# The inverse root of a normalisation on GpSimd by three Newton steps instead of on VectorE, with the sums of squares issued 3 instead of 7 units behind the last products

## The chip, the cores and the metric

The program runs on one core of a Trainium2 chip. A core has a TensorE for matrix products (PE in the profile, its weight loads PEld), VectorE (DVE), ScalarE (ACT), GpSimd (POOL) and SyncE (SP), which here issues every DMA. Each engine works through its own queue in order; an instruction that waits for another engine holds up all that stand behind it on its own. The metric is the device time of one launch in microseconds. Lower is better.

## The reference

Attention by landmarks (Nyström) for 8 batches and 8 heads of 576 tokens with 64 elements, then a normalisation and a gated multi-layer perceptron over the 4608 tokens that come out, all in float32:

```python
def attention(q, k, v):                      # per batch and head
    q_lm, k_lm = means of 18 tokens each     # 32 landmarks
    A, Bm, C = sm(q, k_lm), sm(q_lm, k_lm), sm(q_lm, k)      # softmax, scale 1/8
    Z = Bm.T / (norm_1(Bm) * norm_inf(Bm) + 1e-6)
    for _ in range(6):
        Z = 2 * Z - Z @ Bm @ Z
    return A @ Z @ C @ v

def moe(x, w_gate, w_val, w_out, rms_g):     # x: 4608 x 512, d_ff = 1536
    xn = x / sqrt(mean(x * x, axis=-1) + 1e-6) * rms_g
    g = xn @ w_gate
    return (g * sigmoid(g) * (xn @ w_val)) @ w_out
```

The change is at `1 / sqrt(mean(x * x) + 1e-6)`, one value for each token.

## The kernel before, in words

Each batch `b` (0 to 7, 576 tokens) goes through these stages, written as Python generators that yield between pieces:

- `stage1(b, g)` for the two groups `g` of four heads: VectorE sums landmarks (`lmT`, L342), TensorE makes the scores `sC` and `sA` (a **block** of 32-row matmuls), VectorE takes maxima (L376 to L379) and transposes, ScalarE takes exponentials. Its `back` part makes the rows of A on GpSimd (`tA`, L407 and L414: subtract the maximum, multiply by the inverse sum) and C v on TensorE (`pCV`).
- `newton(b)`: the pseudo-inverse. Six times TensorE multiplies (`pn`) and VectorE updates (`PV`, L498; the last one is `VZ`, L502): a chain that goes to and fro between the two.
- `second(b)`: the attention's output `pO` (the **last products** of the batch), copied by ScalarE to `xr` (L554) and squared (L556). The sums of squares over the 512 channels are matmuls with ones (`pss`, L562), VectorE transposes them (L563), one more matmul adds the four parts (`pms`, L569), and VectorE makes `ms = mean + 1e-6` (L571), a first guess of the inverse root by integer arithmetic (L575, L576), and refines it in **two rounds** of four operations (L578 to L581) on 128 x 18 elements. `Rb` (L583) spreads the root, `Rt` (L585) transposes it, four operations scale `xr` (L587).
- `finish` splits the scaled values into a rounded part `xhi` (ScalarE, L614) and a rest `xlo` (VectorE and GpSimd in turn, L616). A float32 product is made of three fast ones.

The perceptron's first 4 of 12 blocks of 128 hidden channels run while the attention is still going on, in nine **chunks** of 512 tokens (`mlp_chunk`): for each block 12 products `psg` and 12 `psv`, then 48 products `pso` for the output. Chunk `i` needs the split values of batch `i`, and of the batch before for the rest. After the last chunk the other 8 blocks follow in two passes (`Fast`, `unit`), with 7 products in place of 8 for each pair of matrices. Weights are decoded on VectorE and ScalarE from a packed form (L189 to L203).

TensorE's order is the order in which the code issues its matmuls. It is set by `Mixer`, which steps the generators by an estimated clock: each of a chunk's products moves it on by 0.216 units, and a generator that yields `(busy, wait)` goes on when the clock has moved by `busy + wait * slack` (slack 1.8 in the beginning, then 1.3). The constants `OWL0` (batch 0) and `OWL` (the others) are such a wait: between the last products and squares of a batch and its `pss`. On the other engines a scheduler places instructions by its own estimates and by priority. The streams of `second` and `newton` are urgent ones. A chunk is issued only when the batch it needs has been issued in full (`mix.drain`).

Of the kernel before, what the change touches and what calls it, by code (L numbers as in the profile page):

```python
# [13 lines left out]
ALU = mybir.AluOpType  # L14
# [4 lines left out]
P = 128  # L19
# [1 line left out]
NW = 6.0  # L21
NS = 1.0
SLACK0 = 1.8
OWL0 = 7.0
G2 = "newton"
F1 = 1
F2 = 2
# [5 lines left out]
KW2 = 2.5  # L33
OW = 2.0
SQW = 1.5
OWL = 7.0
WW = 2.5
WQ = 0
VM = 0
# [3 lines left out]
RBA = 0  # L43
# [36 lines left out]
def nystrom_moe_kernel(  # L80
# [12 lines left out]
    nc = tc.nc  # L93
# [6 lines left out]
    M = 32  # L100
# [6 lines left out]
    NB = S // M  # L107
# [32 lines left out]
    def mm(*args, **kw):  # L140
        tc.keep_in_program_order(nc.tensor.matmul(*args, **kw))  # L141
# [156 lines left out]
    with tc.tile_pool(name="ap", bufs=1, side="right") as ap, tc.tile_pool(  # L298
# [240 lines left out]
        def second(b):  # L539
            nt = state.pop(b)  # L540
            (Whi, Wlo), ATs = nt["W"], nt["AT"]
            xr = ap.tile([P, NK, S], F32, name="xr", tag="xr", bufs=2)
            sq = ap.tile([P, NK, S], F32, name="sq", tag="sq", bufs=1)
            for g in range(2):
                po = [[pa.tile([P, HS], F32, name="pO", tag="pa") for j in range(2)] for e in range(2)]
                for e in range(2):
                    for n, (w, a) in enumerate(((Whi, 0), (Whi, 1), (Wlo, 0))):
                        for j in range(2):
                            r = slice(j * D, (j + 1) * D)
                            cols = slice(e * HS, (e + 1) * HS)  # L550
                            mm(po[e][j], w[r, g], ATs[g][r, a, cols], start=(n == 0), stop=(n == 2))
                for e in range(2):
                    for j in range(2):
                        nc.scalar.copy(xr[:, 2 * g + j, e * HS : (e + 1) * HS], po[e][j])  # L554
                for kk in (2 * g, 2 * g + 1):
                    nc.scalar.activation(sq[:, kk], xr[:, kk], AF.Square)  # L556
                yield 0.9, ((OWL if b else OWL0) if g == 1 else OW)
            sqT = ap.tile([P, NB, M], F32, name="sqT", tag="sqT", bufs=1)
            for e in range(2):
                pss = pa.tile([P, HS], F32, name="pss", tag="pa")  # L560
                for kk in range(NK):
                    mm(pss[kk * M : (kk + 1) * M, :], ones, sq[:, kk, e * HS : (e + 1) * HS], start=True, stop=True)  # L562
                nc.vector.transpose(  # L563
                    sqT[:, e * (NB // 2) : (e + 1) * (NB // 2), :].rearrange("p n m -> p (n m)"), pss
                )
            yield 1.1, SQW
            part = sqT[:, :, 0]
            pms = pa.tile([P, NB], F32, name="pms", tag="pa")
            mm(pms, sel.rearrange("p g t -> p (g t)"), part, start=True, stop=True)  # L569
            ms = sm.tile([P, NB], F32, name="ms", tag="ms")  # L570
            nc.vector.tensor_scalar(ms, pms, 1.0 / DM, 1e-6, op0=ALU.mult, op1=ALU.add)  # L571
            r1 = sm.tile([P, NB], F32, name="r1", tag="r1")
            r2 = sm.tile([P, NB], F32, name="r2", tag="r2")
            ri = r1.bitcast(I32)
            nc.vector.tensor_single_scalar(ri, ms.bitcast(I32), 1, op=ALU.logical_shift_right)  # L575
            nc.vector.tensor_scalar(ri, ri, -1, 0x5F3759DF, op0=ALU.mult, op1=ALU.add)  # L576
            for c in (1.0, 0.375**2):
                nc.vector.tensor_mul(r2, r1, r1)  # L578
                nc.vector.scalar_tensor_tensor(r2, r2, c, ms, op0=ALU.mult, op1=ALU.mult)
                nc.vector.scalar_tensor_tensor(r2, r2, -10.0 / 3.0, r2, op0=ALU.add, op1=ALU.mult)  # L580
                nc.vector.scalar_tensor_tensor(r1, r2, 5.0, r1, op0=ALU.add, op1=ALU.mult)  # L581
            Rb = ap.tile([P, NB, M], F32, name="Rb", tag="sqT", bufs=1)
            (nc.scalar.mul if RBA else nc.vector.tensor_scalar_mul)(Rb, r1.unsqueeze(2).broadcast_to([P, NB, M]), 0.375**2)  # L583
            Rt = ap.tile([P, S], F32, name="Rt", tag="Rt", bufs=1)
            nc.vector.transpose(Rt, Rb.rearrange("p n m -> p (n m)"))  # L585
            for kk in range(NK):
                last = nc.vector.scalar_tensor_tensor(  # L587
                    xr[:, kk], xr[:, kk], gsb[:, kk : kk + 1], Rt, op0=ALU.mult, op1=ALU.mult
                )
            scaled.append(last.ins)  # L590
            nc.sync.dma_start(x_dram[b], xr)
            xrs[b] = xr
            if HOLD == 2 and b == 0:
                hold.enter_context(tc.issue_after(last.ins))
            finish(b, 0)
            if HOLD == 1 and b == 0:
                hold.enter_context(tc.issue_after(last.ins))
# [4 lines left out]
        def finish(b, which):  # L602
            xr = xrs[b]
            pos = 0
            while pos < S:
                gp = b * S + pos
                i, off = gp // T, gp % T
                n = min(S - pos, T - off)
                if (i > b) != which:
                    pos += n  # L610
                    continue
                xhi, xlo = chunk_tiles(i)
                for kk in range(NK):
                    nc.scalar.copy(xhi[:, kk, off : off + n], xr[:, kk, pos : pos + n])  # L614
                    eng = nc.gpsimd if kk % XLP == XLS else nc.vector
                    eng.tensor_sub(  # L616
                        xlo[:, kk, off : off + n],
                        xr[:, kk, pos : pos + n],
                        xhi[:, kk, off : off + n].bitcast(F32),
                    )  # L620
                pos += n
# [33 lines left out]
        def seconds():  # L655
            for b in range(B):
                while stage["newton"] < b or stage["chunk"] < b - 1:
                    yield -0.3
                yield from second(b)
                stage["second"] = b  # L660
# [393 lines left out]
```

## Time and profile before

| | |
|---|---|
| time, median of 3 runs | 1065.7 us (1065.2 to 1069.69) |
| the profiled execution | 1064.71 us, its span 1062.8 us |
| busy in the span: PE, DVE, ACT, POOL | 993, 743, 487, 90 us |
| granted clock of TensorE, mean | 0.96 |

Times in the profile's views are counted from the start of the span. In the page's strip of 40 slices one slice is 26.6 us and a digit is the busy share in tenths. A row of the timeline gives the start, the time taken, the engine, the source line, the operation, what it writes from what, the shape, and in brackets the idle time of the engine before it with what ended that. Groups give the busy time in total and the mean of one in ns. L141 is the line of the helper that issues every matmul, so that matmuls are told apart by what they write. The last attention batch ends at about 436 us; from there to the end TensorE runs the two passes.

### The profile page before, as it was taken

To read this page: it belongs to the slowest core of one execution; us is meant where nothing else is said; L and a number is where in the kernel's file an instruction comes from. 1 tells how busy PE (TensorE), PEld (TensorE's weight loads), DVE (VectorE), ACT (ScalarE), POOL (GpSimd) and SP (SyncE) were. 2 spreads that over 40 slices of the span, in tenths; PEclk is the share of its full clock that TensorE was granted. 3 is DMA by queue.
4 is the path that set the end of the run, shared out by engine and by line. 5 is a ranking of instruction groups with operands and counts; after the bars stand their busy time and mean duration, and the time that the engine had idled before them with its cause. 6 is when DMAs were issued, how large, how long until landed. Compare 5 with 4: busy or idle time off the path is not lost.

```text
span 1062.8 us, 17582 instructions
## 1 busy us (share of the span) xinstructions
PE 992.8 (93%) x6918; PEld 833.9 (78%) x6918; DVE 743.4 (70%) x1503; ACT 486.7 (46%) x990; POOL 89.5 (8%) x86
## 2 busy tenths in 40 slices
PE   5639689989989999999999999999999999999998
PEld 3326466556767777787989899998999989899997
DVE  7799586797494551988995675747897475675743
ACT  3534556555454543455645352433744334352431
POOL 2243121211020210100000000000000000000000
PEclk7659889999999999999999999999999999999999
DMA  9244343434140211543533505134250432505122
GB/s 335 100 150 136 133 164 105 153 104 163 43 142 11 86 45 40 187 145 119 189 123 135 178 1 179 51 129 155 64 178 21 159 96 83 179 1 178 50 70 80
DMA packets 62946, 123.82 MB, mean 117 GB/s; under 512 B 5520, under 2 KB 27024, under 8 KB 61840
## 3 DMA queue, kind: packets, MB, share of 16 engines
q1 hardware_dynamic: 62864, 122.71, 34.0%
q8 instruction: 54, 0.88, 0.3%
q14 instruction: 28, 0.23, 0.1%
HBM read 84.94 MB, written 37.75 MB: 115 GB/s over the span
## 4 chain that ended last, share of the span: by engine, by line
PE 72%; DVE 15%; DMA 6%; issue 2%; ACT 2%; POOL 2%; SPq 0%; ACTq 0%; POOLq 0%; DVEq 0%
PE pso L141 23%; PE px L141 18%; PE pz L141 9%; PE psg L141 6%; PE psv L141 5%; PE pw L141 5%; DMA qk<-in_q_dram 2%; PE pO L141 2%; DMA srawv<-in_moe_w_val_dram 1%; DVE lmT L342 1%; PE pn L141 1%; DVE xr L587 1%; DVE h L275 1%; PE sC L141 1%; PE pss L141 1%
## 5 line engine op out<-in xcount | busy, mean ns | idle before, releaser
L141 PE MATMUL pso<-whio,h 128*128 128x512 f32 x288 | 96.2, 402 | 5.8 <-DVE h L275 4.7
L141 PE MATMUL pso<-solo,h 128*128 128x512 f32 x432 | 100.4, 390 | 0.0
L829 ACT CAST x<-xf 128x768 fp32r<-128x768 f32 x84 | 68.1, 833 | 69.7 <-DVE xf L847 54.2
L141 PEld LDWEIGHTS pso<-solo,h 128*128 128x128 f32 x432 | 81.0, 188 | 16.3
L141 PE MATMUL pso<-sowhio,h 128*128 128x512 f32 x288 | 90.9, 390 | 0.0
L141 PE MATMUL psg<-xhi,whig 128*128 128x512 f32 x144 | 60.7, 421 | 25.6 <-ACT xhi L614 25.6
L945 DVE TENSOR_TENSOR ob<-ob,pso 128x512 f32<-128x512 f32 x72 | 48.8, 684 | 49.1 <-PE pso L141 48.1
L830 DVE TENSOR_TENSOR x<-xf,x 128x768 fp32r<-128x768 f32 x84 | 79.2, 953 | 5.0 <-ACT x L829 5.0
L877 DVE TENSOR_TENSOR h<-c,h 128x384 fp32r<-128x384 f32 x96 | 53.2, 555 | 37.3 <-ACT h L876 37.2
L898 ACT COPY c<-px 128x384 f32<-128x384 f32 x48 | 23.1, 481 | 108.6 <-PE px L141 108.6
L141 PEld LDWEIGHTS pso<-whio,h 128*128 128x128 f32 x288 | 53.4, 188 | 20.4 <-DVE h L275 6.0
L876 ACT CAST h<-c 128x384 fp32r<-128x384 f32 x96 | 49.4, 515 | 34.5 <-DVE c L887 28.3
L141 PE MATMUL psg<-xlo,whig 128*128 128x512 f32 x144 | 60.6, 421 | 4.7 <-DVE xlo L616 4.0
L141 PEld LDWEIGHTS pso<-sowhio,h 128*128 128x128 f32 x288 | 54.1, 188 | 11.0
L141 PE MATMUL psg<-xhi,wlog 128*128 128x512 f32 x144 | 60.5, 420 | 0.0
L141 PE MATMUL psv<-xhi,wlov 128*128 128x512 f32 x144 | 58.1, 403 | 0.0
L141 PE MATMUL px<-x,swfs0c 128*128 128x384 f32 x288 | 58.0, 335 | 0.0
L141 PE MATMUL psv<-xlo,whiv 128*128 128x512 f32 x144 | 58.0, 403 | 0.0
L141 PE MATMUL px<-x,swfs1c 128*128 128x384 f32 x288 | 57.8, 334 | 0.1
L141 PE MATMUL px<-x,swfs2c 128*128 128x384 f32 x288 | 57.8, 335 | 0.0
L141 PE MATMUL psv<-xhi,whiv 128*128 128x512 f32 x144 | 57.8, 401 | 0.0
L141 PE MATMUL pso<-wloo,h 128*128 128x512 f32 x144 | 57.4, 398 | 0.0
(224 smaller groups left out, 2231.6 us busy)
## 6 DMA issues: line engine op xcount, KB each, us to landing
xd<-xr SPq DMA_DIRECT2D x8, 1152.0 KB, 4.3
pd<-ob SPq DMA_DIRECT2D x36, 256.0 KB, 2.1
xf<-xd SPq DMA_DIRECT2D x8, 1152.0 KB, 7.5
ob<-pd SPq DMA_DIRECT2D x36, 256.0 KB, 3.5
pe<-ob SPq DMA_DIRECT2D x36, 256.0 KB, 2.6
ob<-pe SPq DMA_DIRECT2D x36, 256.0 KB, 2.8
out_dram<-ob SPq DMA_DIRECT2D x36, 256.0 KB, 2.7
vt<-in_v_dram SPq DMA_DIRECT2D x16, 512.0 KB, 4.0
```

The costliest lines, as they stand in the source:

```text
L141: tc.keep_in_program_order(nc.tensor.matmul(*args, **kw))
L275: nc.vector.tensor_sub(h2, s, h1.bitcast(F32))
L342: nc.vector.tensor_reduce(lmT[:, z], qk[z].rearrange("p h (m c) -> p h m c", c=LM), axis=AX.X, op=ALU.add)
L587: last = nc.vector.scalar_tensor_tensor(xr[:, kk], xr[:, kk], gsb[:, kk : kk + 1], Rt, op0=ALU.mult, op1=ALU.mult)
L829: nc.scalar.copy(t[:, 0], src)
L830: nc.vector.tensor_sub(t[:, 1], src, t[:, 0].bitcast(F32))
L876: nc.scalar.copy(hi, s)
L877: nc.vector.tensor_sub(lo, s, hi.bitcast(F32))
L898: nc.scalar.copy(c1, px)
L945: nc.vector.tensor_add(ob, ob, bank.pop(t))
```

## The change

The two rounds on VectorE become three Newton steps on GpSimd, each of four operations, `y = y * (1.5 - 0.5 * ms * y * y)`, twelve in a row where each needs the one before. Rounds of the old kind carried a factor that `Rb` multiplied in; the new ones don't, so `Rb` is a plain copy. `OWL0` and `OWL` go from 7 to 3.

```diff
-OWL0 = 7.0
+OWL0 = 3.0
-OWL = 7.0
+OWL = 3.0
...
             nc.vector.tensor_single_scalar(ri, ms.bitcast(I32), 1, op=ALU.logical_shift_right)
             nc.vector.tensor_scalar(ri, ri, -1, 0x5F3759DF, op0=ALU.mult, op1=ALU.add)
-            for c in (1.0, 0.375**2):
-                nc.vector.tensor_mul(r2, r1, r1)
-                nc.vector.scalar_tensor_tensor(r2, r2, c, ms, op0=ALU.mult, op1=ALU.mult)
-                nc.vector.scalar_tensor_tensor(r2, r2, -10.0 / 3.0, r2, op0=ALU.add, op1=ALU.mult)
-                nc.vector.scalar_tensor_tensor(r1, r2, 5.0, r1, op0=ALU.add, op1=ALU.mult)
+            for _ in range(3):
+                nc.gpsimd.tensor_mul(r2, r1, r1)
+                nc.gpsimd.tensor_mul(r2, r2, ms)
+                nc.gpsimd.tensor_scalar(r2, r2, -0.5, 1.5, op0=ALU.mult, op1=ALU.add)
+                nc.gpsimd.tensor_mul(r1, r1, r2)
             Rb = ap.tile([P, NB, M], F32, name="Rb", tag="sqT", bufs=1)
-            (nc.scalar.mul if RBA else nc.vector.tensor_scalar_mul)(Rb, r1.unsqueeze(2).broadcast_to([P, NB, M]), 0.375**2)
+            nc.vector.tensor_copy(Rb, r1.unsqueeze(2).broadcast_to([P, NB, M]))
```

Both edits move instructions on all engines, since the first changes what the scheduler has to place and the second when the planner issues it. Three places matter.

TensorE, behind the sums of squares of batch 0. Lines with + stand there after the change, lines with - before. `psg` are the first products of chunk 0.

```order
 L141 MATMUL sC<-lmT 32x32 x4
 L141 MATMUL pss<-sq,ones 32x288 x8
+L141 MATMUL pms<-sqT,sel 128x18
+L141 MATMUL psg<-xhi_704,whig_433 128x512
+L141 MATMUL psg<-xlo_705,whig_433 128x512
+L141 MATMUL psg<-xhi_704,wlog_434 128x512
```

The second block of scores of batch 1 stood between `pss` and `pms`; now it stands behind 19 products of chunk 0. With batch 1 it is the same: before, a block of batch 2 stood between its `pss` and its `pms`, and now `pms` and chunk 1 follow `pss` at once. In both orders that `pss` stands behind all 48 `pso` of chunk 0.

VectorE, from `ms` of batch 0 on (`r` is the root, `w` a weight that is being decoded, `ss`, `mx`, `sumA`, `rA` are of the attention of batch 1). Before:

```order
L571 TENSOR_SCALAR ms<-pms 128x18
L379 TENSOR_TENSOR mx<-mx,nscale 128x2
L410 TENSOR_REDUCE sumA<-tA 128x18
L575 TENSOR_SCALAR r_775<-ms 128x18
L191 TENSOR_SCALAR w_820<-w_820 128x512
L576 TENSOR_SCALAR r_775<-r_775 128x18
L411 TENSOR_SCALAR sumA<-sumA 128x18
L389 TENSOR_TENSOR ss<-ss 128x1
L578 TENSOR_TENSOR r_776<-r_775 128x18
L413 RECIPROCAL rA<-sumA 128x18
L579 SCALAR_TENSOR_TENSOR r_776<-r_776,ms 128x18
L390 TENSOR_SCALAR ss<-ss 128x2
```

and now:

```order
L571 TENSOR_SCALAR ms<-pms 128x18
L379 TENSOR_TENSOR mx<-mx,nscale 128x2
L191 TENSOR_SCALAR w_728<-w_728 128x512
L575 TENSOR_SCALAR r_679<-ms 128x18
L190 TENSOR_SCALAR w_764<-w_764 128x512
L576 TENSOR_SCALAR r_679<-r_679 128x18
L194 SCALAR_TENSOR_TENSOR w_728<-wrawg_726,w_728 128x512
L389 TENSOR_TENSOR ss<-ss 128x1
L191 TENSOR_SCALAR w_764<-w_764 128x512
L390 TENSOR_SCALAR ss<-ss 128x2
L197 SCALAR_TENSOR_TENSOR w_728<-wrawg_726,w_728 128x512
L583 COPY Rb<-r_679 128x576
```

Before, 20 more rows follow ahead of `Rb`. Now `Rb` is the twelfth, and it waits there for GpSimd.

VectorE, from `ms` of batch 2 on (`PV` belongs to the pseudo-inverse of batch 3, `tA`, `sumA` and `qk` to later scores). Before, the first round of the root; the second follows and then `Rb`:

```order
L571 TENSOR_SCALAR ms<-pms 128x18
L419 TENSOR_TENSOR AS<-AT,AS 128x576
L575 TENSOR_SCALAR r_2277<-ms 128x18
L576 TENSOR_SCALAR r_2277<-r_2277 128x18
L578 TENSOR_TENSOR r_2278<-r_2277 128x18
L502 SCALAR_TENSOR_TENSOR VZ<-PV,pn 128x2x64
L579 SCALAR_TENSOR_TENSOR r_2278<-r_2278,ms 128x18
L580 SCALAR_TENSOR_TENSOR r_2278<-r_2278 128x18
```

and now, from the end of the first guess:

```order
L576 TENSOR_SCALAR r_2231<-r_2231 128x18
L392 TENSOR_SCALAR Bm<-eb,rs 128x32
L413 RECIPROCAL rA<-sumA 128x18
L342 TENSOR_REDUCE lmT<-qk_2302 128x64
L498 SCALAR_TENSOR_TENSOR PV<-PV,pn 128x192
L416 STREAM_TRANSPOSE AT<-tA 128x576
L583 COPY Rb<-r_2231 128x576
L498 SCALAR_TENSOR_TENSOR PV<-PV,pn 128x192
L585 STREAM_TRANSPOSE Rt<-Rb 128x576
L419 TENSOR_TENSOR AS<-AT,AS 128x576
L498 SCALAR_TENSOR_TENSOR PV<-PV,pn 128x192
L587 SCALAR_TENSOR_TENSOR xr<-xr,gsb,Rt 128x576 x4
```

Where the chain of the pseudo-inverse had ended (`VZ`) before the root was made, three of its updates now stand around and behind `Rb`. On GpSimd one `tA` product (L414) stands behind the third of the twelve operations of batch 2; in batch 1 a `tA` subtraction (L407) stands ahead of all twelve. ScalarE's order has 32 loads of activation tables where it had 22, since exponentials and the perceptron's activations alternate more often.

## Prediction

> **What bounds the kernel now.** I read the page's busy shares first, then the strip, to see where TensorE is not full:
>
> ```profile
> PE 992.8 (93%) x6918; PEld 833.9 (78%) x6918; DVE 743.4 (70%) x1503; ACT 486.7 (46%) x990; POOL 89.5 (8%) x86
> PE   5639689989989999999999999999999999999998
> DVE  7799586797494551988995675747897475675743
> ```
>
> From the slice at 440 us to the end TensorE is full, and the change puts nothing there. What it can move is the 70 us that TensorE stands idle, nearly all ahead of 440 us. The waits of TensorE, summed, name one reason for a third of it, and the timeline has the waits one by one:
>
> ```profile
> PE psg L141 <- ACT xhi L614: 25.6, 3, 13.9
> ...
> 67.14 0.80 PE L141 MATMUL psg<-xhi,whig 128*128 128x512 f32 x1 [13.93 <-ACT xhi L614]
> 134.06 0.79 PE L141 MATMUL psg<-xhi,whig 128*128 128x512 f32 x1 [11.26 <-ACT xhi L614]
> 137.73 0.80 PE L141 MATMUL psg<-xlo,whig 128*128 128x512 f32 x1 [1.82 <-DVE xlo L616]
> 200.59 0.50 PE L141 MATMUL psg<-xhi,whig 128*128 128x512 f32 x1 [0.44 <-ACT xhi L614]
> 201.90 0.50 PE L141 MATMUL psg<-xlo,whig 128*128 128x512 f32 x1 [0.81 <-DVE xlo L616]
> 239.88 0.43 PE L141 MATMUL sA<-qk,lmT 64*32 64x288 f32 x1 [3.16 <-DVE PV L443]
> 437.10 0.73 PE L141 MATMUL pso<-whio,h 128*128 128x512 f32 x2 [1.32 <-DVE h L275]
> ```
>
> Chunks 0, 1 and 2 each begin by waiting for the normalised batch, 13.9, 11.3 and 0.4 us; from chunk 3 on nothing waits for it. So three boundaries pay for the chain from `pss` to `xhi`, and the last only just. The windows show what else is full there: VectorE.
>
> ```profile
> 60.00:80.00 20.00, 10.83 (x65) 7.53 (x66) 17.96 (x35) 7.74 (x15) 11.18 (x8) 0.57 0.42 145
> 120.00:140.00 20.00, 6.93 (x69) 4.48 (x62) 19.51 (x56) 11.09 (x28) 6.76 (x7) 0.62 0.49 176
> 220.00:240.00 20.00, 16.84 (x246) 10.63 (x251) 19.89 (x47) 10.70 (x19) 5.30 (x5) 1.00 0.33 117
> ```
>
> The columns are the length, then the busy time of PE, PEld, DVE, ACT, POOL. The timeline of VectorE gives the chain of batch 0, and that of batch 4, where nothing stands between:
>
> ```profile
> 48.20 0.97 DVE L563 STREAM_TRANSPOSE sqT<-pss 128x288 f32<-128x288 f32 x2 [0.60 <-PE pss L141]
> 49.23 0.74 DVE L406 TENSOR_REDUCE mA<-tA 128x18 f32<-128x576 f32 x1
> 53.24 0.18 DVE L571 TENSOR_SCALAR ms<-pms 128x18 f32<-128x18 f32 x1
> 55.67 1.13 DVE L580 SCALAR_TENSOR_TENSOR r<-r 128x18 f32<-128x18 f32 x1
> 62.26 0.44 DVE L583 TENSOR_SCALAR Rb<-r 128x576 f32<-128x576 f32 x1
> 63.37 0.76 DVE L585 STREAM_TRANSPOSE Rt<-Rb 128x576 f32<-128x576 f32 x1
> 65.63 2.99 DVE L587 SCALAR_TENSOR_TENSOR xr<-xr,gsb,Rt 128x576 f32<-128x576 f32 x4
> ...
> 289.90 0.18 DVE L576 TENSOR_SCALAR r<-r 128x18 int32<-128x18 int32 x1
> 291.82 0.46 DVE L583 TENSOR_SCALAR Rb<-r 128x576 f32<-128x576 f32 x1
> ```
>
> From `ms` to `Rb` it takes 9.0 us in batch 0, where other work stands between the links, and 1.7 us from the end of L576 in batch 4.
>
> **The price of a GpSimd link.** The trace has no 18-element operation on GpSimd. It has these (groups by shape, then the timeline):
>
> ```profile
> L616 POOL TENSOR_TENSOR xlo<-xr,xhi 128x64 fp32r<-128x64 f32 x4 | 2.9, 718 | 33.0 <-ACT xhi L614 33.0
> L131 POOL MEMSET nscale<- 128x1 f32 x1 | 0.1, 100 | 0.0
> ...
> 30.73 1.26 POOL L203 TENSOR_TENSOR wlog<-w,whig 128x512 fp32r<-128x512 f32 x1 [4.77 <-ACT whig L202]
> 50.12 1.16 POOL L407 TENSOR_TENSOR tA<-tA,mA 128x576 f32<-128x576 f32 x1 [5.43 <-DVE mx L379]
> 55.19 1.58 POOL L414 TENSOR_TENSOR tA<-tA,rA 128x576 f32<-128x576 f32 x1 [3.92 <-DVE ss L390]
> 346.71 0.60 POOL L616 TENSOR_TENSOR xlo<-xr,xhi 128x192 fp32r<-128x192 f32 x1 [1.08 <-ACT xhi L614]
> ```
>
> 1.26 us for 512 and 0.60 for 192 elements make 2.06 ns an element, so 0.60 - 174 x 0.00206 = 0.24 us for 18. Between dependent links comes a gap: on VectorE nine steps from L576 to `Rb` took 1.92 us, 0.21 each for operations of 0.18, a gap of 0.03 to 0.04; from the end of `mA` (49.97) to L407 (50.12) it was 0.15. I take 0.09, so 0.33 a link and 4.0 us for twelve. The bounds are 0.14 (the MEMSET's 0.10 and the small gap: 1.7 us) and 0.87 (the mean 128x64, during which VectorE was busy, and the large gap: 10.4 us). I stay near the line because VectorE itself falls idle behind `Rb`.
>
> The other engine suffers too: L580 took 1.13 us and ended at 56.80, when L414 (55.19 + 1.58 = 56.77) ended. The Trainium skill, SBUF — State Buffer, section "Who interferes with whom", says that a VectorE instruction with two inputs in SBUF and a GpSimd instruction that reads SBUF use one port pair, which the first to issue holds for its whole instruction, while the other stands still. That row agrees, and the rule speaks against this change: a link that meets a two-input VectorE operation would wait it out (the sum would be the second rival's), and only where none meets one does the sum of this part hold.
>
> **First boundary (chunk 0).** `pms` now follows `pss`, so `ms` comes right behind `sqT` (49.17) at 50.0 instead of 53.24. With four decode operations of some 0.35 between, L576 ends near 51.2; the chain ends at 55.3; `Rb` 0.4, an L194 of 0.6, `Rt` 0.7 and the first `xr` 0.75 give 57.8, and `psg` starts near 58.5, not 67.14: 8.6 us earlier. It is not all kept. The block of scores and its transposes, 2 us of TensorE hidden in the wait, now stand in the open. It bears on the rest of the chunk how full VectorE is:
>
> ```profile
> 41.34 0.68 DVE L197 SCALAR_TENSOR_TENSOR w<-wrawv,w 128x512 int32<-128x512 int32 x1
> 51.55 0.41 DVE L190 TENSOR_SCALAR w<-w 128x512 f32<-128x512 f32 x1
> 76.30 0.75 DVE L410 TENSOR_REDUCE sumA<-tA 128x18 f32<-128x576 f32 x1 [2.04 <-ACT tA L408]
> 105.08 0.69 DVE L271 TENSOR_TENSOR s<-s,psv 128x512 f32<-128x512 f32 x1 [1.12 <-PE psv L141]
> 106.45 0.69 DVE L275 TENSOR_TENSOR h<-s,h 128x512 fp32r<-128x512 f32 x1 [0.69 <-ACT h L274]
> ```
>
> VectorE has the same work up to the last `h` of chunk 0 (106.45), less eight root operations and one L197 of 0.68 (1.7 us); with the 0.60 ahead of L563 and smaller ones it was idle for some 5 us between 48 and 107 and can use that, but now stands idle 2.5 us at `Rb`, since the five operations behind L576 last 2 us and the chain 4. So VectorE allows 4.3, TensorE 6.6: I take **-5** (-7.5 to -2).
>
> **Second boundary (chunk 1).** `pss` stands behind all 48 `pso` in both orders: the shorter distance moves nothing here, since `newton` of batch 1 is issued later. I count from the start of `pss`, which was at:
>
> ```profile
> 119.68 0.69 PE L141 MATMUL pss<-sq,ones 128*32 128x288 f32 x8
> ...
> 189.45 0.94 PE L141 MATMUL pss<-sq,ones 128*32 128x288 f32 x12
> ```
>
> Chunk 1 was going at 137.73, 18.05 later. Now: maxima and transposes of the block just ahead (1.15), `sqT` 0.85, `mA` 0.7, L407 on GpSimd ahead of the chain (until 4.1), chain to 8.1, `Rb`, `Rt`, then a landmark sum L342 of 1.3 ahead of `xr` (10.5), four `xr` 3.1, `xlo` 0.6: 14.3. That is 3.7 less, but a block and transposes, 2.0 us, are again in the open: **-1.7** (-3.5 to +0.7).
>
> **Third boundary (chunk 2).** From `pss` (0): `sqT` done at 1.9; then a landmark sum whose load is issued only behind the block that frees its buffer, 1.8 earlier:
>
> ```profile
> qk<-in_q_dram SPq DMA_DIRECT2D x14, 576.0 KB, 4.3
> ```
>
> so it starts at 2.5 and `PV` follows at 3.8. `pms` 4.8, `ms` 5.3, L576 5.9; three links, 7.0; L414 of 1.16, 8.2; nine links, 11.1. In order behind `Rb` come `PV`, `Rt`, L419, `PV`: 13.5; four `xr` and `xlo`: 17.0. TensorE has 8.9 us for that time (19 `pso` of 0.227, five `pn` of 0.5, `pss`, `pms`, transposes). It idles 7.9 instead of 1.25: **+6.6** (+3.5 to +10). Here the cover that hid the chain, 12.45 us from 189.45 to 201.90, is gone because the last products come later in chunk 1.
>
> **Chunk 2 and batch 3.** The third `pn` behind `pms` needs a `PV` that stands behind `Rb`: `ms` at 4.0, L576 at 5.4, chain to 9.5, `Rb`, L342, `PV` at 11.6, where TensorE is ready at 8.4: +3.2. The wait of 3.16 for `PV` L443 at 239.88 should go, as that `pCV` is now issued well before its block: **0** (-2 to +3). **Batches 4 to 7**: the chain is 2.3 us longer but ends ahead of its chunk; its cover is 24 products or more (5.4 us); uncovered it would be 2.3 each. Chunk 7's chain comes a block earlier, which takes away the 1.32 at 437.10: **-1.3**.
>
> Sum: -5 - 1.7 + 6.6 + 0 - 1.3 = -1.4 against the profiled 1064.7. The median of the runs is 1.0 above that, so 1065.7 - 1.4 = **1064.3 us**. Within 0.5% (5.3 us) counts as no change.
>
> **Rivals.**
> *The links are cheap.* At 0.15 a link the chain is 1.8 us: the first two boundaries give -7 and -2.7, the third costs 3.5, batch 3 gives -1.5: -9, 1057 us. For it: the MEMSET's 0.10. Against: the slope of the real two-input rows. It decides below some 0.25 a link (four places x 12 links x 0.08 = 3.9 on top of -1.4).
> *The links wait for VectorE* (slower). Where a link meets a decode or transpose of 0.4 to 0.8 us, it takes 0.5 rather than 0.33: 6 us for twelve, +2 at each of four places: 1064.3 + 8 = 1072 us. For it: the 128x64 mean of 718 ns, twice the line's 0.33, and L414's 1.58 against 1.16. Against: VectorE stops at `Rb`. It decides above 0.47.
> *Table loads.* Ten more loads in ScalarE's order:
>
> ```profile
> L270 ACT ACT_TABLE_LOAD x11 | 14.1, 1283 | 3.5 <-PE psg L141 3.3
> ```
>
> 1.28 each; the four extra ones of chunk 0, if each stood on the way to an `h`, would eat the first term: 1064.3 + 5 = 1069 us. Against: ScalarE is busy for 7.74 of the 20 us from 60 on.
>
> **How the numbers follow.** The forecast has 0.45, cheap links 0.25, waiting links 0.22, table loads 0.08. Cheap links are nearly all of faster (with a bit of the forecast's spread, 0.25), waiting links and part of the loads of slower (0.25), the rest 0.50. The range, 1055 to 1075, reaches over both sides; the forecast's own is 1059 to 1070.
>
> **What would show it.** Right: first `psg` near 58, chunk 1 going 14 us after its `pss`, chunk 2 17 us after, with TensorE waiting some 8 us there; L578 to L581 on POOL start 0.33 apart; VectorE idle before L583, put down to POOL. Wrong: starts 0.2 or 0.5 apart, no wait at chunk 2, or the gain of chunk 0 gone by the first `pss` of batch 1 (forecast near 114).

## The result and the profile after

The changed kernel takes 1074.56 us (median of 6 runs, 1073.46 to 1075.28), against 1068.87 us for the kernel before in the same runs: a ratio of 1.0061, 95% interval 1.0042 to 1.0079. By the ratio it is slower by some 6.5 us, where 1.4 us less and "no change" was forecast. Profile against profile it is 1072.4 us of span against 1062.8, 9.6 us more; the profiled execution of the kernel before, of 1064.71 us, was 4.2 below its median, so some 3 us of the 9.6 belong to this pair of executions and not to the two kernels.

The page of the changed kernel, busy shares and the strip of TensorE:

```profile
PE 997.3 (93%) x6918; PEld 833.5 (78%) x6918; DVE 731.9 (68%) x1439; ACT 498.2 (46%) x1000; POOL 112.0 (10%) x182
PE   5568599789989999999999999999999999999998
```

VectorE lost 11.5 us of work and GpSimd got 22.5, but TensorE stands idle for 75.1 us instead of 70.0, and the same 6918 matmuls keep it busy for 4.5 us longer. Its waits for the normalised batch in the timeline of the changed kernel, and four from 300 us on:

```profile
59.64 0.79 PE L141 MATMUL psg<-xhi,whig 128*128 128x512 f32 x1 [10.07 <-ACT xhi L614]
127.62 0.80 PE L141 MATMUL psg<-xhi,whig 128*128 128x512 f32 x1 [9.30 <-ACT xhi L614]
197.47 0.80 PE L141 MATMUL psg<-xhi,whig 128*128 128x512 f32 x1 [2.33 <-ACT xhi L614]
200.74 0.80 PE L141 MATMUL psg<-xlo,whig 128*128 128x512 f32 x1 [2.48 <-DVE xlo L616]
307.57 0.30 PE L144 MATMUL sF<-ident,E 128*64 128x128 f32 x1 [3.60 <-DVE tA L395]
359.36 0.50 PE L141 MATMUL pso<-whio,h 128*128 128x512 f32 x1 [0.65 <-ACT s L270]
442.96 0.50 PE L141 MATMUL pso<-whio,h 128*128 128x512 f32 x1 [0.80 <-ACT h L274]
477.68 0.50 PE L141 MATMUL pso<-whio,h 128*128 128x512 f32 x1 [1.31 <-ACT h L274]
```

The first two waits are shorter than before (13.9 and 11.3), and the third was 0.44. From 300 us on the kernel before had two waits of more than 1 us, the 1.32 at 437.10 and this one:

```profile
306.46 0.73 PE L141 MATMUL pso<-whio,h 128*128 128x512 f32 x2 [2.50 <-DVE h L275]
```

The last four of the changed kernel do not name the normalised batch at all: they name a transpose of scores (`tA` L395) and the activations of the chunk that is running (`s`, `h`).

How far the changed kernel was ahead or behind (-: earlier than before), and how much more or less TensorE had idled by then, by windows that end at the same events:

| event | before, us | after, us | difference | difference of idle time so far |
|---|---|---|---|---|
| first product of chunk 0 | 67.14 | 59.64 | -7.5 | -4.9 |
| `pss` of batch 1 | 119.68 | 115.94 | -3.7 | -3.5 |
| chunk 1 going (first `xlo` product) | 137.73 | 129.75 | -8.0 | -5.2 |
| `pss` of batch 2 | 189.45 | 182.14 | -7.3 | -5.8 |
| chunk 2 going | 201.90 | 200.74 | -1.2 | +0.9 |
| chunk 3 | 268.76 | 271.93 | +3.2 | +1.3 |
| chunk 4 | 317.54 | 327.94 | +10.4 | +3.0 |
| chunk 5 | 365.84 | 373.42 | +7.6 | +4.2 |
| chunk 7 | 443.60 | 450.17 | +6.6 | +3.6 |
| chunk 8 | 476.24 | 485.03 | +8.8 | +4.9 |
| end of the span | 1062.8 | 1072.4 | +9.6 | +5.1 |

(The order of the work differs between two rows, so the idle time says more than the difference; at chunk 8 and the end all work ahead is the same.)

The price of a link is seen in batch 4, from VectorE's and GpSimd's timelines:

```profile
287.02 0.18 DVE L576 TENSOR_SCALAR r<-r 128x18 int32<-128x18 int32 x1
290.87 0.46 DVE L583 COPY Rb<-r 128x576 f32<-128x576 f32 x1 [3.67 <-POOL r L581]
...
287.28 0.22 POOL L578 TENSOR_TENSOR r<-r 128x18 f32<-128x18 f32 x1 [17.14 <-DVE r L576]
287.57 0.23 POOL L579 TENSOR_TENSOR r<-r,ms 128x18 f32<-128x18 f32 x1
...
290.61 0.23 POOL L581 TENSOR_TENSOR r<-r,r 128x18 f32<-128x18 f32 x1
```

An operation takes 0.22 us, and the next starts 0.30 us after it did. Twelve take 3.6 us. From the end of L576 to `Rb` it is 3.7 us, where it was 1.7 before; VectorE does nothing in them. Over the eight batches it stands for 19.4 us in front of `Rb`, in the waits of the changed kernel:

```profile
DVE Rb L583 <- POOL r L581: 19.4, 8, 3.7
```

### The profile page after: what moved, and what is told of

The parts are those of the page before. It is cut to its first block, busy times and chain, and to the rows that moved or that the text cites. A ratio compares the mean times of both kernels' runs of the same rounds, so it can differ in the third digit from the quotient of the medians.

```text
span 1072.4 us, 17633 instructions
## 1 busy us (share of the span) xinstructions
PE 997.3 (93%) x6918; PEld 833.5 (78%) x6918; DVE 731.9 (68%) x1439; ACT 498.2 (46%) x1000; POOL 112.0 (10%) x182
## 4 chain that ended last, share of the span: by engine, by line
PE 67%; DVE 16%; DMA 7%; issue 4%; POOL 3%; ACT 3%; SPq 0%; ACTq 0%; POOLq 0%; DVEq 0%
PE pso L141 23%; PE px L141 17%; PE pz L141 9%; PE psg L141 5%; PE pw L141 4%; PE psv L141 4%; DMA qk<-in_q_dram 2%; DVE xr L587 2%; PE pO L141 1%; DMA srawv<-in_moe_w_val_dram 1%; DVE lmT L342 1%; PE pn L141 1%; DMA srawo<-in_moe_w_out_dram 1%; DVE h L275 1%; DVE sw L732 1%
## 5 line engine op out<-in xcount | busy, mean ns | idle before, releaser
L141 PE MATMUL pso<-whio,h 128*128 128x512 f32 x288 | 98.9, 410 | 3.6 <-ACT h L274 2.3
```

## The experiments

Twelve kernels ran, each beside the kernel before on the same chip, in 5 to 12 executions. Three words recur. The **distances** are `OWL0` and `OWL`. The **links** are the operations that refine the root. The **orders** are those in which ScalarE, VectorE and GpSimd issue everything else; the scheduler chooses them anew after each edit.

### The parts of the change, one at a time

`newton_only`: the root on GpSimd, distances 7. `owl_only`: distances 3, the root on VectorE. `owl0_only` and `newton_owl0`: only batch 0's distance is 3, with the root on VectorE and on GpSimd.

```diff
-OWL0 = 7.0
+OWL0 = 3.0          # owl_only, owl0_only, newton_owl0
-OWL = 7.0
+OWL = 3.0           # owl_only
-            for c in (1.0, 0.375**2):
+            for _ in range(3):       # newton_only, newton_owl0: L577 to L583 of the change
```

> The root on GpSimd as in the change, the distances left at 7, so TensorE's order is that of the kernel before. Theory 'order' (the loss comes from issuing the sums of squares earlier: chunk 2 loses its cover, ScalarE's and VectorE's orders change): ratio 0.996 to 1.002 to the kernel before; first psg at about 61 in place of 67.14, the wait for psg of chunk 2 grows by about 2 us at most. Theory 'links' (the loss is the longer chain on GpSimd at every boundary): ratio 1.004 to 1.008, with TensorE's waits for xhi longer at chunks 1 and 2.

> Both distances at 3, the root still on VectorE, so TensorE's order is that of the changed kernel. Theory 'order': ratio 1.004 to 1.008, with 5 to 8 us of TensorE idle between pss of batch 2 and chunk 2. Theory 'links': ratio 0.996 to 1.001, with 4 us or less idle there.

> Only the distance of batch 0 at 3, the root on VectorE. Theory 'order': chunk 0 starts 4 to 6 us earlier and most of it stays, since nothing is moved in chunk 1: ratio 0.996 to 0.999. Theory 'links': the distance does nothing by itself, ratio 0.999 to 1.001.

> The root on GpSimd and only the distance of batch 0 at 3. Theory 'order': chunk 0 starts at 59.6 as in the changed kernel and chunk 2 keeps its cover: ratio 0.994 to 0.999, below both kernels. Theory 'links': ratio 1.003 to 1.007, as the changed kernel.

| kernel | links | distances | ratio to before | 95% interval |
|---|---|---|---|---|
| owl0_only | VectorE | 3, 7 | 1.0019 | 1.0003 to 1.0035 |
| newton_only | GpSimd | 7, 7 | 1.0049 | 1.0034 to 1.0064 |
| owl_only | VectorE | 3, 3 | 1.0065 | 1.0045 to 1.0086 |
| newton_owl0 | GpSimd | 3, 7 | 1.0091 | 1.0073 to 1.0109 |
| the change | GpSimd | 3, 3 | 1.0061 | 1.0042 to 1.0079 |

Neither theory stands. The links alone and both distances alone each cost about as much as all together, and the kernel that should have been the best of all is the worst. TensorE's order is the same in kernels with the same distances, so something else that each edit brings must weigh as much as the edits: the orders.

The first suspicion was ScalarE. In `newton_only` it has 26 table loads instead of 22; ahead of chunk 5 a silu (`s` L270) stands behind exponentials of the next batch, with three loads around them, and TensorE waits there for 3.57 us where it waited for nothing. So the orders were taken out of the question.

### The orders held

Each engine was made to issue its instructions in the order of another kernel, by an edge for issue order from each instruction to the next (the call is shortened here); only the links remain free:

```diff
+    for a, b in zip(order, order[1:]):      # order: the engine's order in the other kernel
+        tc.add_manual_dep(own[b], own[a].name, NoSync, reason="pin")
```

`newton_pinA` is `newton_only` with ScalarE in the order of the kernel before; `newton_pinAV` has VectorE and GpSimd held too; `before_pinAV` is the kernel before with the orders of `newton_only`; `newton6_pinAV` is `newton_pinAV` with 24 links:

```diff
-            for _ in range(3):
+            for _ in range(6):
```

> The root on GpSimd, distances 7, and ScalarE's instructions held to the order that they have in the kernel before (22 table loads instead of 26). Theory 'ScalarE's order' (with the links on GpSimd the scheduler puts a silu of chunks 3, 4 and 6 behind exponentials of the next batch, with two more table loads, and the products wait for that h): TensorE's waits for pso of those chunks go back to 2.5, 0 and 1.3 us, and the ratio to the kernel before is 0.995 to 1.001. Theory 'links' (the chain on GpSimd itself is what is late): the waits stay at 1.7 + 2.5, 3.6 and 0.5 + 2.6, ratio 1.003 to 1.007.

> As newton_pinA, and all other instructions of VectorE and GpSimd held to the order of the kernel before too, so that nothing but the twelve links moves. Theory 'ScalarE's order': ratio 0.997 to 1.002, with chunk 0 and 1 starting no more than 3 us apart from the kernel before. Theory 'links': 1.003 to 1.007.

> The reverse: the root stays in two rounds on VectorE, but ScalarE, VectorE and GpSimd issue everything else in the order of newton_only (26 table loads). Theory 'ScalarE's order': slower without one link on GpSimd, ratio 1.003 to 1.008, with the waits of 3 to 4 us for pso of chunks 4 and 6. Theory 'links': ratio 0.999 to 1.002.

> newton_pinAV with six Newton steps, 24 links instead of 12: the chain grows by 12 x 0.30 = 3.6 us in each batch, all else in the same order. If a link on the path costs what it takes at the boundaries that wait (chunks 0, 1 and 2): 3 x 3.6 = 10.8 us above newton_pinAV, and up to 3 us more where it reaches a later chunk (ratio to newton_pinAV 1.008 to 1.014). If the chain is covered by other work at the boundaries: less than 4 us above it (1.000 to 1.004).

| kernel | links | orders of | median, us | ratio to before | 95% interval |
|---|---|---|---|---|---|
| before_pinAV | VectorE | newton_only | 1061.59 | 0.9939 | 0.9920 to 0.9958 |
| newton_only | GpSimd | its own | 1072.89 | 1.0049 | 1.0034 to 1.0064 |
| newton_pinAV | GpSimd | before | 1077.66 | 1.0090 | 1.0069 to 1.0111 |
| newton_pinA | GpSimd | ScalarE as before | 1080.69 | 1.0116 | 1.0097 to 1.0134 |
| newton6_pinAV | GpSimd, 24 | before | 1113.20 | 1.0425 | 1.0402 to 1.0449 |

The theory of ScalarE's order falls twice. With 22 loads again the kernel is slower still (1.0116), and the orders of `newton_only`, with their 26 loads, are faster than the original ones as soon as the links are back on VectorE (0.9939, the fastest of all kernels here, ahead of both that were given). Orders held, the links alone cost 9.5 us (1077.66 against 1068.12) with the old orders and 1.0049 / 0.9939 = 1.011, some 11 us (1072.89 against 1061.59), with the new ones. The doubling asks the same of every batch: 12 more links should take 3.6 us, and the kernel takes 35.5 us longer, 4.4 us a batch. That is more than the 10.8 to 14 that the expectation had for the boundaries that wait. In the two profiles each chunk falls back by another 2.9 to 5.7 us, so the added links are in the open in **all** batches, with something on top. In its waits the activations of the running chunk have come up beside the boundaries:

```profile
PE psg L141 <- ACT xhi L615: 37.1, 3, 17.9
PE pso L141 <- DVE h L276: 9.3, 6, 3.1
PE pso L141 <- ACT h L275: 6.3, 3, 4.2
PE pso L141 <- DVE s L272: 3.3, 2, 2.2
```

(In the held kernels a line added ahead shifts all numbers behind it by one.)

With 12 links the place is another. Between `newton_pinAV` and the kernel before chunk 2 starts 0.9 us later and chunk 8 11.1; between `newton_only` and `before_pinAV` it is 1.4 and 10.9. So the three boundaries that the forecast priced pay little for the longer chain, and the chunks behind them pay nearly all.

What lies between a longer chain and an activation can be read from the pair with the same orders. Batch 5, first in `before_pinAV`, its timeline on VectorE, ScalarE and TensorE, and a window behind the wait:

```profile
331.20 0.18 DVE L572 TENSOR_SCALAR ms<-pms 128x18 f32<-128x18 f32 x1 [2.15 <-PE pms L141]
334.80 0.46 DVE L584 TENSOR_SCALAR Rb<-r 128x576 f32<-128x576 f32 x1
342.85 0.12 DVE L380 TENSOR_TENSOR mx<-mx,nscale 128x2 f32<-128x2 f32 x1
...
343.05 1.28 ACT L383 ACT_TABLE_LOAD   x1 [1.80 <-DVE mx L380]
347.00 0.60 ACT L271 ACTIVATE s<-psg 128x512 f32<-128x512 f32 x1
...
347.65 0.50 PE L141 MATMUL pso<-whio,h 128*128 128x512 f32 x1 [1.81 <-ACT s L271]
```

```profile
350.00:355.00 5.00, 5.00 (x73) 3.56 (x72) 4.14 (x9) 3.55 (x10) 3.35 (x3) 1.00 0.30 110
```

and in `newton_only`:

```profile
337.55 0.18 DVE L571 TENSOR_SCALAR ms<-pms 128x18 f32<-128x18 f32 x1 [2.15 <-PE pms L141]
342.91 0.46 DVE L583 COPY Rb<-r 128x576 f32<-128x576 f32 x1 [2.83 <-POOL r L581]
350.97 0.12 DVE L379 TENSOR_TENSOR mx<-mx,nscale 128x2 f32<-128x2 f32 x1
...
351.17 1.28 ACT L382 ACT_TABLE_LOAD   x1 [1.80 <-DVE mx L379]
355.12 0.60 ACT L270 ACTIVATE s<-psg 128x512 f32<-128x512 f32 x1
...
355.76 0.50 PE L141 MATMUL pso<-whio,h 128*128 128x512 f32 x1 [3.57 <-ACT s L270]
```

```profile
355.00:360.00 5.00, 4.24 (x14) 3.10 (x14) 3.42 (x11) 4.74 (x9) 0.00 (x0) 0.67 0.01 3
```

From `ms` to `Rb` it is 3.60 us in the one and 5.36 in the other, 1.76 more. Everything that VectorE has queued behind `Rb` comes 1.76 us later, the maxima `mx` of the next batch among it (8.05 us behind `Rb` in one kernel, 8.06 in the other); the exponentials wait for them, the running chunk's `s` stands behind the exponentials on ScalarE, and TensorE's wait for it grows from 1.81 to 3.57, by 1.76. So here the chain is not late for the chunk that it feeds. It is late for what stands behind it on VectorE's queue. Nor is that all: in the 5 us that follow the clock that TensorE is granted is 0.67 in the second kernel and 1.00 in the first. From `pss` of batch 5 to chunk 5 it is 33.5 and 36.8 us, 3.3 more, of which the wait explains 1.76.

### The same for the change as a whole

`owl_pinAV` is the changed kernel with the root on VectorE again and its own orders held. `after2_pinAV` is the changed kernel with two Newton steps, its orders held. `owl_from2` has distances of 3 only from batch 2 on. `owl0_pinAV` is `newton_owl0` with the root on VectorE, orders held.

```diff
-            for _ in range(3):
+            for _ in range(2):                                       # after2_pinAV
-                yield 0.9, ((OWL if b else OWL0) if g == 1 else OW)
+                yield 0.9, ((7.0 if b < 2 else OWL) if g == 1 else OW)   # owl_from2
```

> The changed kernel with its root back in two rounds on VectorE: distances 3, and ScalarE, VectorE, GpSimd and SyncE issue all else in the order of the changed kernel. Theory 'exposed chain' (each link on GpSimd lengthens every batch, here as with distances of 7, where the same pair differed by 11 us): 5 to 12 us faster than the changed kernel, ratio to the kernel before 0.995 to 1.002. Theory 'hidden by the new distances' (with 3, the chain is covered): within 2 us of the changed kernel, ratio 1.004 to 1.008.

> The changed kernel with two Newton steps instead of three (the root is less exact; the third step is left out), all else in the same order. Theory 'exposed chain': four links of 0.30 less in each of eight batches, 9.6 us if all of it counts, so 4 to 10 us faster than the changed kernel. Theory 'hidden by the new distances': within 2 us of it.

> Batch 0's distance 3, the others 7, the root on VectorE, and the orders of newton_owl0 on all engines. Theory 'exposed chain': 8 to 13 us faster than newton_owl0 (1.0091), ratio 0.995 to 1.002. Theory 'orders' (what differs between these kernels comes from the scheduler's orders): within 3 us of newton_owl0.

> Distances of 3 from batch 2 on, batches 0 and 1 as before, the root on VectorE. Theory 'given back' (chunk 2 loses its cover because an earlier chunk 1 pushes the last products of batch 2 to its end, not because of batch 2's own distance): TensorE idles 2 us or less between pss of batch 2 and the first xlo product of chunk 2 (7.3 with all distances at 3). Theory 'own distance': 5 us or more. The time itself depends on the scheduler's orders too: 0.994 to 1.006.

| kernel | links | orders of | ratio to before | 95% interval |
|---|---|---|---|---|
| owl_pinAV | VectorE, 8 | the change | 0.9985 | 0.9970 to 1.0000 |
| after2_pinAV | GpSimd, 8 | the change | 0.9992 | 0.9971 to 1.0013 |
| the change | GpSimd, 12 | the change | 1.0061 | 1.0042 to 1.0079 |
| owl0_pinAV | VectorE, 8 | newton_owl0 | 0.9961 | 0.9945 to 0.9977 |
| newton_owl0 | GpSimd, 12 | newton_owl0 | 1.0091 | 1.0073 to 1.0109 |
| owl_from2 | VectorE, 8 | its own | 1.0034 | 1.0016 to 1.0051 |

Eight links on GpSimd cost no more than eight on VectorE, as far as this tells (the intervals overlap); the last four cost 7.4 of the 8.1 us between the change and `owl_pinAV`. The new distances do not hide the chain: 1.0061 / 0.9985 is 1.0076, 8.1 us, where the pairs with other distances gave 1.0090, 1.011 and 1.013.

This pair shows in the change itself what batch 5 showed above. From chunk 3 to chunk 8 TensorE idles 7.7 us in the change and 3.1 in `owl_pinAV`. By chunk 3 it had idled 3.1 more already (61.5 against 58.3). In batch 4 `ms` is written 0.2 us earlier in the change, and `Rb` starts 1.75 later (290.87 against 289.12), the table load ahead of the next exponentials 1.73 later (300.39 against 298.66), the transposed scores `tA` 1.70 later, and TensorE's wait for them grows by 1.65, from the 1.95 of `owl_pinAV` to the 3.60 shown at 307.57:

```profile
289.12 0.46 DVE L584 TENSOR_SCALAR Rb<-r 128x576 f32<-128x576 f32 x1
305.37 0.44 DVE L396 STREAM_TRANSPOSE tA<-sA 128x288 f32<-128x288 f32 x1
305.87 0.30 PE L144 MATMUL sF<-ident,E 128*64 128x128 f32 x1 [1.95 <-DVE tA L396]
```

What the distances do is seen between pairs with the links on VectorE. From `pss` of batch 2 to the going of chunk 2, TensorE idles 1.3 us in the kernel before, 1.5 in `before_pinAV`, 7.3 in `owl_only` and 6.8 in `owl_pinAV`, whose timeline has

```profile
194.40 0.79 PE L141 MATMUL psg<-xhi,whig 128*128 128x512 f32 x1 [2.33 <-ACT xhi L615]
197.68 0.79 PE L141 MATMUL psg<-xlo,whig 128*128 128x512 f32 x1 [2.49 <-DVE xlo L617]
```

and 8.0 in the changed kernel. So nearly all of the new stall at chunk 2 is the distances' and not GpSimd's. `owl_from2` was to tell whether it comes from batch 2's own distance or from the earlier chunk 1. It idles 4.8 us there, between the two expectations, and the waits for `psg` are gone; what it waits for is another thing that stands behind `xr` on VectorE:

```profile
203.72 0.65 PE L141 MATMUL pCV<-vt,ET 128*32 128x64 f32 x32 [3.53 <-DVE Wlo L521]
```

That question stays open.

Put in a row, the change is three steps. The distances alone: 1.0065 (`owl_only`). The orders that the scheduler makes once the links are gone from VectorE: 0.9985 / 1.0065, 0.8% faster. The links on GpSimd: 1.0076. The middle step was seen three times, with the same sign: 0.6% from the kernel before to `before_pinAV`, 0.6% from `owl0_only` to `owl0_pinAV`. Why those orders are better was not tried, and no kernel was held to its own orders, so what the holding does by itself is not shown.

## Why the prediction was wrong

**The price of a link: right.** 0.33 us forecast, 0.30 measured; 3.6 us for twelve against 4.0. The line through the two-input operations was the better guide than the MEMSET.

**First boundary: -5 forecast, -3.5 measured** (idle time up to `pss` of batch 1). Chunk 0 started at 59.64 against 58.5. In batch 0 two links met two-input decode operations of VectorE (0.59 and 0.60), and the copy met a GpSimd product:

```profile
50.77 0.59 POOL L578 TENSOR_TENSOR r<-r 128x18 f32<-128x18 f32 x1 [6.12 <-DVE r L576]
...
55.16 1.26 POOL L203 TENSOR_TENSOR wlog<-w,whig 128x512 fp32r<-128x512 f32 x1
55.23 1.50 DVE L583 COPY Rb<-r 128x576 f32<-128x576 f32 x1 [2.83 <-POOL r L581]
```

0.59 in place of 0.22, and 1.50 in place of 0.46 for `Rb`, which ends 0.3 us behind L203. For the links this is the lock of the Trainium skill, SBUF — State Buffer, section "Who interferes with whom", and the trace agrees. In batches 4 to 7, where VectorE waits 1.6 to 3.7 us for the links, all 48 take 0.21 to 0.23. So the rival that rested on it was dear in batch 0 only; of the links behind it one was long, 0.64 in batch 3.

**Second boundary: right.** 14.3 us from `pss` to the going of chunk 1 forecast, 13.8 measured; idle time 1.7 us less, as forecast.

**Third boundary: right in sum and in mechanism.** 17.0 us forecast, 18.6 measured; 7.9 us of idle time forecast, 8.0 measured; L414 did stand between the links and took 1.16. The runs add that this stall comes with the new distances, which took the cover away, and not with GpSimd: `owl_only` has 7.3 of it.

**Batches 4 to 7: the step that failed.** "The chain is 2.3 us longer but ends ahead of its chunk" is right (1.9 longer in batch 4) and beside the point: none of these chunks waited for it. The step looked for who needs the chain's result, and left out who stands behind the chain's *consumer* on its engine. `Rb` waits for GpSimd at the head of VectorE's queue, and the maxima of the next scores, and through ScalarE the activations of the running chunk, wait with it. The timeline before had shown that these were on the edge: the 2.50 us at 306.46 and the 1.32 at 437.10 were waits for `h` already, and the second was booked as a gain of 1.3. Idle time from chunk 3 to chunk 8 grew by 3.7 us (1.3 to 4.9), where -1.3 was forecast; against `owl_pinAV`, with the same orders, the links make it 4.6.

**The term that was not there: the clock.** The sum counted waits alone. TensorE's busy time rose by 4.5 us with the same matmuls. The mean clock hides it, 0.962 after and 0.961 before: in both profiles the clock is 0.50 for 82 us in all. But TensorE is busy for 47.4 of them now and was for 40.4, and 7 more busy us at half the clock are 3.5 of the 4.5. In the changed kernel the windows around chunk 2 have

```profile
180.00:200.00 20.00, 12.73 (x161) 7.58 (x149) 15.19 (x37) 8.83 (x22) 6.66 (x16) 0.91 0.34 113
200.00:220.00 20.00, 18.15 (x178) 11.81 (x178) 15.70 (x37) 10.29 (x24) 4.55 (x5) 0.84 0.39 149
```

a clock of 0.91 and then 0.84 around the stall, where the kernel before has 1.00 and 0.91 in the same windows, and the pair of batch 5 showed 1.6 us lost in this way behind a wait of 3.57. The length of one wait does not decide it. The wait of 2.5 us of the kernel before, at 306.46, left the clock at 1.00, in that kernel's windows:

```profile
305.00:310.00 5.00, 3.46 (x50) 2.12 (x50) 5.00 (x19) 1.51 (x3) 2.01 (x3) 1.00 0.14 52
```

but in `newton_only` one of 2.50 that ends at 303.71, 3.2 us behind one of 1.69, lies in a stretch from 302 to 308 us with a clock of 0.51. These are single executions. `owl_pinAV` is 8 us faster than the change by the ratios, idles less (67.6 us against 75.1), and its TensorE is busy for longer (998.7 against 997.3), so the clock's part of the loss in the medians is not shown.

Idle time came out at +5.1 where -1.4 was forecast: +1.5 of the difference from chunk 0, some 5 from batches 4 to 7, the rest small terms of both signs. With the 4.5 us of busy time this is the 9.6 us of the profiles.

**The rivals.** Cheap links (0.15) fell at the first row of GpSimd. Waiting links were right in sign and size (1072), but by luck, since the mechanism was wrong: the links seldom waited for VectorE, VectorE waited for the links. Table loads: 32 as the order had said, but their number does not order the kernels, since `before_pinAV` has 26 and is the fastest, and `newton_pinA` has 22 and is slower than the change.

What no part of the prediction had is that an edit re-deals the orders of the other engines, at up to 0.8% here. Those orders were read at three places; what they were worth elsewhere was not visible ahead of a run.

## What to carry to other kernels

Moving a chain to an idle engine makes its consumer wait at the head of another engine's queue. So ask what is queued behind that consumer, in every stage where the chain runs, and not only who needs the result. A chain that gets hardly longer may move for nothing: with eight links it was 2.5 us from L576 to `Rb` in batches 4 to 7, against 1.7 to 2.4 on VectorE. What it is longer by beyond that can count in each repetition, and more where the stall also brings down TensorE's clock. Where a scheduler places the instructions, hold its order fixed on both sides before believing what a small edit costs: here the orders alone were worth as much as the edit, with the other sign.

## What the runs showed of the hardware that was not expected

- A dependent chain of 18-element operations runs on GpSimd at 0.30 us a step (0.22 and a gap of 0.08), against 0.21 on VectorE (0.18 and a gap of 0.03): the operation itself takes hardly longer.
- A stall of TensorE can be paid again by its clock: behind a wait of 3.57 us in `newton_only` it was 0.67 for the next 5 us. Behind one of 2.50 us it stayed at 1.00 in the kernel before, and in `newton_only` it was 0.51 from 302 to 308 us, around one of 2.50 us that followed one of 1.69.
- A VectorE copy of one input took 1.50 us beside a GpSimd product (`Rb` beside L203, which had started 0.07 us earlier) and 0.46 in the other seven batches. The product took 1.26 us, as it does at 30.73 in the kernel before.
